# First half of k as fp32 with casts on chip, and one w_out product one slot earlier

## The chip, the cores and the metric

The kernel runs on one core of a Trainium2 chip. The metric is the device time of one execution in microseconds; for several runs the median is given. A profile is one execution, recorded with the start and length of every instruction and of every DMA packet.

## The reference

The input is q, k and v of shape (8, 8, 576, 64) in fp32 (batch, heads, sequence, head dimension), a w_in of 512 x 2048 and a w_out of 2048 x 512.

```
scores = q @ k^T / 8, kept where |i - j| <= 32, else -1e9
attn   = softmax(scores) @ v              # per batch and head
x      = attn as (8*576, 8*64)            # 4608 tokens of 512
h      = x @ w_in
g      = h if h >= 1;  0 if h <= -1;  else (h + 1)^2 / 4
out    = g @ w_out                        # fp32
```

## The kernel before

**Types and layout.** Everything that TensorE (PE) reads is bf16. Almost all loads are issued by GpSimd (POOL), whose DMAs change fp32 to bf16 on the way. The first half of q (`q32`) is the exception: SyncE (SP) and ScalarE (ACT) issue one DMA each for one group of four heads, as fp32, and `cast` (L338) makes bf16 of it on chip: VectorE (DVE) the first 5 of 9 columns of rows (L342), ACT the other 4 (L343), into one tile `qb` with both head groups side by side. `load_half` (L80) loads one half of one of q or k of batch 0 for one group of heads; without an engine given it is POOL's, and a tile `qh` or `kh` in bf16 is the result.

**Attention.** PE transposes q and k to `qT` and `kT`, in parts of five and four columns: a tile from `cast` takes 9 transposes at full width (L189), one from POOL 18 at half width (L187). Part 0 is copied out of PSUM by ACT, part 1 by DVE (L190). `scores` (L211) adds the band's mask by products of an identity with a bias (L206), multiplies blocks of keys with their window of queries (L227) and takes the Exp on ACT (L235). `sums` (L265) multiplies the result with ones and with v (L293); its `end()` takes Ln and Exp(-x) on ACT for the reciprocal (L299, L300), and DVE multiplies into `xT` (L305, for the last 96 tokens of a batch L308).

**The MLP.** Time runs in slots `a` (L482): slot a does 256 tokens (t = a // 8) by 256 columns of w_in (f = a % 8) into one `hp` of PSUM (L504). Tile `hp` has two buffers, and slot 6 takes one of `ps_o`. ACT makes `rr` (L508), then in the slots of `two_on_act` (1 and 7 to 12) also its square (L512), and DVE writes `gT` from hp (L513); in the others DVE does both steps (L515, L516). The products with w_out of the first two blocks of 256 tokens (p = 0, 1) are cut into 16 `pair`s (L452): pair x does half of w_out's columns (x // 8) with 4 of 16 rows of blocks (x % 4) in 16 products of 128 x 256 (L460; 8 for each 128 tokens). Their first ten places are written by hand in the list `pairs` (L378), as (slot, pair); the other parts go by `quarter` (L444), one for each slot.

**The start.** All comes in program order on each engine. POOL issues: the first half of k (two DMAs), an affine_select for the identity and the band (L131), v of batch 0 (four DMAs), w_in in pieces, the second half of q and k, more of w_in with the first part of w_out, three copies for masks, the rest of w_out's first 256 columns (L155: rows of blocks 4 to 7, then 8 to 15), then rows of batch 1 for q and k (`load_rows`), v of batch 1, and so on. PE: 11 products of zeros (`keep_warm`, L336), transposes of q, transposes of k, 3 warm products, three groups of scores, 4 warm products, the first sums, 2, the second sums, 7, then slot 0. ACT and DVE: the casts of q, the copies of qT, the copies of kT, and ACT the Exps. The second half of q and k is transposed in slot 1 (`tposes`, L323), and its scores come in slots 2 and 3.

Of the kernel before, what the change touches and what calls it, by code (L numbers as in the profile page):

```python
# [7 lines left out]
FP = mybir.dt.float32  # L8
# [6 lines left out]
def kernel(  # L15
# [19 lines left out]
    nc = tc.nc  # L35
    B, H, S, D = q.shape
# [40 lines left out]
    qn, kn, vn = {}, {}, {}  # L77
    HD = (slice(0, 64), slice(64, 128))

    def load_half(half, t, h, eng=None, x=None):  # L80

        src, dst, nm = ((q, qn, "qh"), (k, kn, "kh"))[t]
        if (0, half) not in dst:
            dst[0, half] = early.tile([128, 2, S], BF, name=nm, tag=nm, bufs=2) if x is None else x
        (eng or nc.gpsimd).dma_start(out=dst[0, half][:, h], in_=src[0].rearrange(
            "(h y) (l p j) d -> h l p y (j d)", h=2, l=2, p=32)[h][half])
# [29 lines left out]
                            in_=moe_w_out.rearrange("(ko ki) f -> ki ko f", ki=128)[:, k0:k1, 256 * c:256 * c + 256])  # L116

    early = ctx.enter_context(tc.tile_pool(name="early", bufs=1))
    q32 = early.tile([128, 2, S], FP, name="q32")
    for h in range(2):  # L120
        load_half(0, 0, h, (nc.sync, nc.scalar)[h], q32)
    for h in range(2):
        load_half(0, 1, h)
    A.preload_act_table_set("natural_log_exp_and_others")
    warm = const.tile([128, 512], BF, name="warm")
    V.memset(warm, 0.0)
# [15 lines left out]
    def put(todo):  # L142
        for fn, *x in todo:
            fn(*x)
# [7 lines left out]
    for m, n, x in ((mask4, 8, 128), (mask8, 4, TAIL)):  # L152
        P.tensor_copy(m.rearrange("p (n j) -> p n j", n=n),
                      band[:, :x].rearrange("p (n j) -> p n j", n=1).to_broadcast([128, n, x]))
    put([(load_w_out, 0, 4, 8), (load_w_out, 0, 8, 16)] + [(load_rows, 1, t) for t in range(2)])  # L155
    put([(load_v, 1, n) for n in range(4)] + [(load_w_out, 1, 8 * n, 8 * n + 8) for n in range(2)])
    put([(load_nat, 2, t) for t in range(2)] + [(load_v, 2, n) for n in range(4)])

# [3 lines left out]
    def qkT(b, t):  # L162
        if t == 0:
            return qTs[b % 3][:, PAD:]
        if b not in kT:
            kT[b] = ktp.tile([128, NY * S], BF, name="kT")
        return kT[b]

    def tpose(b, n, t, copy, ps):


        half, part = divmod(n, 2)
        j0, j1 = ((0, 5), (5, 9))[part]
        if b:
            src = qn[b] if t == 0 else kn[b]
            src = [src[:, half + 2 * h] for h in range(2)]
            dst = qkT(b, t).rearrange("d (y e p j) -> d y e p j", y=2, e=2, j=9)[:, half, :, :, j0:j1]
            like = "d j (e p) -> d e p j"
        else:
            src = (qn, kn)[t][b, half]  # L180
            src = src if src.shape[1] == 9 else [src[:, h] for h in range(2)]
            dst = qkT(b, t).rearrange("d (y l p j) -> d l y p j", l=2, p=32, j=9)[:, half, :, :, j0:j1]
            like = "d j (p y) -> d y p j"
        for j in range(j0, j1):
            if isinstance(src, list):
                for h in range(2):
                    nc.tensor.transpose(ps[HD[h], j - j0], src[h][:, D * j:D * j + D], ident)  # L187
            else:
                nc.tensor.transpose(ps[:, j - j0], src[:, j], ident)  # L189
        return lambda: copy(dst, ps[:, :j1 - j0].rearrange(like, p=64 if b else 32))  # L190
# [20 lines left out]
    def scores(b, ys, pars, cs, eng, pool=ps_s, w=128):  # L211

        if b not in pt:
            pt[b] = ptp.tile([128, 2, 2, 2, 512], BF, name="pt")
        ps = two_banks(pool)
        n = 0
        if eng is None:
            cols = (ys[1] - ys[0]) * (pars[1] - pars[0]) * (cs[1] - cs[0])
            add_mask([ps[:, h] for h in range(2)], cols, w)
        for y1 in range(*ys):  # L220
            for par in range(*pars):
                for c2 in range(*cs):
                    c = 2 * c2 + par
                    for a in range(2):
                        for h in range(2):
                            s0 = S * (y1 + 2 * a) + 64 * c
                            nc.tensor.matmul(ps[HD[a], h, w * n:w * n + w], kT[b][HD[h], s0:s0 + 64],  # L227
                                             qTs[b % 3][HD[h], PAD + s0 - 32:PAD + s0 - 32 + w],
                                             start=eng is not None, stop=True, skip_group_check=True)
                    n += 1  # L230
        p = pt[b][:, :, ys[0]:ys[1], pars[0]:pars[1], 128 * cs[0]:128 * cs[1] - 128 + w]
        m = 2 if n > cs[1] - cs[0] else 1
        p = p[:, :, ys[0] - ys[0]] if ys[1] - ys[0] == 1 else p[:, :, :, 0]
        like = "p h (y j) -> p h y j"
        A.activation(p, ps[:, :, :w * n].rearrange(like, y=m), AF.Exp, scale=D ** -0.5)  # L235
        mask(eng, p, mask4[:, :256 * n].rearrange("p (h j) -> p h j", h=2).rearrange(like, y=m))
# [81 lines left out]
    def tp1(pool):  # L318
        if pool is ps_h:
            return pool.tile([128, 8, 128], BF, name="tp", tag="hp")  # L320
        return pool.tile([128, 2, 8, 128], BF, name="tp", tag="bb")[:, 0]
# [10 lines left out]
    def keep_warm(n, pool, tag):  # L332

        z = pool.tile([128, 512], FP, name="z", tag=tag)
        for _ in range(n):
            nc.tensor.matmul(z, warm[:, :128], warm, start=True, stop=True)  # L336

    def cast(x, nm, cut):  # L338

        y = early.tile([128, 9, 2, D], BF, name=nm)  # L340
        o, i = y.rearrange("p j h d -> p h j d"), x.rearrange("p h (j d) -> p h j d", d=D)
        V.tensor_copy(o[:, :, :cut], i[:, :, :cut])  # L342
        A.copy(o[:, :, cut:], i[:, :, cut:])  # L343
        return y.rearrange("p j h d -> p j (h d)")

    with tc.tile_pool(name="ps_p", bufs=1, space=bass.MemoryType.PSUM) as ps_p:
        keep_warm(11, ps_h, "hp")

        V.memset(qkT(0, 0).rearrange("d (y s) -> d y s", y=NY)[:, :, S // 2:352], 0.0)
        for b in range(LONG):  # L350
            V.memset(qkT(b, 0).rearrange("d (y s) -> d y s", y=NY)[:, :, S - PAD:], 0.0)
        V.memset(qkT(0, 1).rearrange("d (y s) -> d y s", y=NY)[:, :, S // 2:320], 0.0)
        qn[0, 0] = cast(q32, "qb", 5)
        qq = [tpose(0, n, 0, (A.copy, V.tensor_copy)[n], tp1(ps_h)) for n in range(2)]
        for x in qq:
            x()
        kk = [tpose(0, n, 1, (A.copy, V.tensor_copy)[n], tp1((ps_n, ps_p)[n])) for n in range(2)]
        keep_warm(3, ps_h, "hp")
        for x in kk:
            x()  # L360
        scores(0, (0, 1), (0, 2), (0, 2), None)
        scores(0, (0, 2), (0, 1), (2, 3), None, ps_n, 32)
        scores(0, (1, 2), (0, 2), (0, 2), None, ps_p)
        keep_warm(4, ps_h, "hp")
        e0 = sums(0, 0, 0, TB)
        keep_warm(2, ps_h, "hp")
        e1 = sums(0, 1, 0, TB, ps_p)
        keep_warm(7, ps_h, "hp")
        e0()
        e1()  # L370
# [4 lines left out]

    NB = NT // TB
    NF = DFF // 256
    pairs = [(6, 0), (8, 1), (9, 2), (10, 3), (11, 4), (12, 5), (15, 6), (15, 8), (16, 7), (17, 9)]  # L378
    two_on_act = (1, 7, 8, 9, 10, 11, 12)
    ev = {}  # L380

# [100 lines left out]
    for a in range(NF * NB + NF):  # L482
        t, f = divmod(a, NF)
# [70 lines left out]
```

## Time and profile before

| | us |
|---|---|
| median of 4 runs | 309.04 (308.52 to 309.59) |
| the profiled execution | 308.60 |
| its span (first to last instruction) | 306.8 |
| PE busy | 299.3 (98%) |
| DVE, ACT, POOL busy | 241.9 (79%), 192.4 (63%), 76.8 (25%) |
| chain that ended last: PE's share | 90% |
| fp32 halves of q, issue to landing | 3.6 and 4.3 |
| kh (POOL, 144 KB each), issue to landing, of four | 4.5 to 5.8 |
| granted TensorE clock | full, throughout |

How to read it: a row of the timeline gives start, length, engine, line, what is written and read, and in brackets the idle time of the engine before it with what ended that. The chain of waits is followed back from the last instruction; each piece starts when the piece before it releases it. PEld is the loading of weights, which runs beside PE. DMA packets of POOL are counted by what they write, in bf16.

### The profile page before, as it was taken

What the parts mean: (1) busy time and instruction counts of PE and PEld (TensorE: products, weight loads), DVE (VectorE), ACT (ScalarE), POOL (GpSimd) and SP (SyncE); (2) the same over time, 40 slices, a digit from 0 to 9 for tenths busy, and PEclk for the clock granted to TensorE, in tenths of its full rate; (3) what the DMA queues carried; (4) which work ended last, traced back from release to release, by engine and by line L of the source; (5) the groups of instructions that cost most, each with busy time, mean ns of one, the idle gap of its engine ahead of it and who ended that gap; (6) DMA issues with size and microseconds to landing.
All of it is one profiled execution on the core that took longest, in us unless ns stands there. A gap on an engine that the chain in (4) does not pass through costs nothing.

```text
span 306.8 us, 8495 instructions
## 1 busy us (share of the span) xinstructions
PE 299.3 (98%) x3650; PEld 206.3 (67%) x3650; DVE 241.9 (79%) x376; ACT 192.4 (63%) x320; POOL 76.8 (25%) x91
## 2 busy tenths in 40 slices
PE   7989999999999999999999999999999999999995
PEld 3467878876666666666666666666666666666654
DVE  4278568888888888889888888889888888888760
ACT  4688786738856667666656666566676666554431
POOL 8798451037009106400550002800000000000000
PEclk9999999999999999999999999999999999999999
DMA  9999999999999999996899154990810011010111
GB/s 153 184 197 199 182 201 152 169 156 157 138 191 99 177 172 102 162 93 142 105 167 140 34 112 104 141 157 19 177 49 36 34 36 36 35 36 34 60 45 68
DMA packets 137157, 35.70 MB, mean 116 GB/s; under 512 B 122144, under 2 KB 132896, under 8 KB 137120
## 3 DMA queue, kind: packets, MB, share of 16 engines
q0 software_dynamic: 102960, 18.06, 82.8%
q1 hardware_dynamic: 34016, 16.81, 24.4%
q8 instruction: 28, 0.46, 0.6%
q10 hardware_dynamic: 144, 0.29, 0.4%
q14 instruction: 9, 0.07, 0.1%
HBM read 36.70 MB, written 9.44 MB: 150 GB/s over the span
## 4 chain that ended last, share of the span: by engine, by line
PE 90%; ACT 3%; DVE 2%; DMA 2%; POOL 1%; issue 1%; POOLq 0%; ACTq 0%
PE hp L504 39%; PE op L444 36%; PE bb L293 6%; PE op L460 4%; PE bb L227 2%; DMA vn<-in_v_dram 2%; PE op L433 1%; ACT pt L235 1%; POOL vn L106 1%; PE tp L187 1%; DVE xT L305 1%; ACT rc L300 1%; ACT lr L299 1%; DVE mx L515 0%; ACT rr L508 0%
## 5 line engine op out<-in xcount | busy, mean ns | idle before, releaser
L504 PE MATMUL hp<-xT,w_in 128*128 128x256 bf16 x1152 | 149.6, 273 | 1.5 <-DMA w_in<-in_moe_w_in_dram 0.6
L508 ACT ACTIVATE rr<-hp 128x512 f32<-128x512 f32 x144 | 85.6, 594 | 87.9 <-PE hp L504 87.9
L504 PEld LDWEIGHTS <-w_in 128*128 128x128 bf16 x1152 | 112.0, 98 | 41.2 <-issue 1.6
L444 PE MATMUL op<-w_out,gT 128*128 128x512 bf16 x496 | 126.9, 380 | 0.0
L515 DVE TENSOR_TENSOR mx<-hp,rr 128x512 f32<-128x512 f32 x137 | 94.5, 689 | 30.9 <-ACT rr L508 28.9
L516 DVE SCALAR_TENSOR_TENSOR gT<-rr,mx 128x512 bf16<-128x512 f32 x137 | 95.2, 695 | 4.7
L444 PEld LDWEIGHTS <-gT 128*128 128x128 bf16 x496 | 46.1, 98 | 34.8
L98 POOL DMA_DIRECT2D qn<-in_q_dram x12 | 14.6, 1222 | 113.2 <-DMA kT<-kn 109.5
L235 ACT ACTIVATE pt<-bb 128x1024 bf16<-128x1024 f32 (+1 forms) x33 | 32.7, 1001 | 4.9 <-PE bb L227 3.6
L305 DVE TENSOR_TENSOR xT<-bb,rc 128x512 bf16<-128x512 f32 (+1 forms) x32 | 21.0, 657 | 10.2 <-ACT rc L300 9.7
L106 POOL DMA_DIRECT2D vn<-in_v_dram x32 | 27.5, 900 | 3.4 <-DMA w_out<-in_moe_w_out_dram 3.4
L300 ACT ACTIVATE rc<-lr 128x512 f32<-128x512 f32 (+2 forms) x40 | 23.5, 587 | 1.3
L449 ACT COPY osb<-op 128x512 f32<-128x512 f32 x31 | 18.0, 582 | 8.7 <-PE op L444 8.3
L299 ACT ACTIVATE lr<-bb 128x512 f32<-128x512 f32 (+2 forms) x40 | 22.1, 552 | 0.5 <-PE bb L293 0.4
L201 DVE TENSOR_TENSOR pt<-pt,mask 128x1024 bf16<-128x1024 bf16 (+1 forms) x33 | 20.2, 614 | 0.5 <-ACT pt L235 0.5
L293 PE MATMUL bb<-pt,ones 64*64 64x256 bf16 (+3 forms) x352 | 19.6, 256 | 0.1
L293 PE MATMUL bb<-pt,vn 64*64 64x128 bf16 (+3 forms) x712 | 18.4, 204 | 0.3 <-DMA vn<-in_v_dram 0.3
L293 PEld LDWEIGHTS <-vn 64*64 64x64 bf16 x712 | 16.7, 107 | 0.5 <-DMA vn<-in_v_dram 0.5
L460 PE MATMUL op<-w_out,gT 128*128 128x256 bf16 x128 | 16.5, 273 | 0.0
L293 PEld LDWEIGHTS <-ones 64*64 64x64 bf16 x352 | 10.2, 105 | 8.9 <-issue 8.9
L98 POOL DMA_DIRECT2D kn<-in_k_dram x12 | 14.6, 1232 | 0.6 <-DMA vn<-in_v_dram 0.3
L227 PE MATMUL bb<-qT,kT 64*64 64x128 bf16 (+1 forms) x520 | 13.1, 217 | 0.2 <-DVE kT L190 0.2
(59 smaller groups left out, 113.1 us busy)
## 6 DMA issues: line engine op xcount, KB each, us to landing
out_dram<-osb SPq DMA_DIRECT2D x35, 256.0 KB, 2.4
vn<-in_v_dram POOLq DMA_DIRECT2D x32, 144.0 KB, 10.5
qn<-in_q_dram POOLq DMA_DIRECT2D x12, 288.0 KB, 6.8
kn<-in_k_dram POOLq DMA_DIRECT2D x12, 288.0 KB, 9.4
w_in<-in_moe_w_in_dram POOLq DMA_DIRECT2D x12, 128.0 KB, 5.8
w_out<-in_moe_w_out_dram POOLq DMA_DIRECT2D x3, 512.0 KB, 15.2
kh<-in_k_dram POOLq DMA_DIRECT2D x4, 144.0 KB, 5.1
qn<-in_q_dram POOLq DMA_DIRECT2D x1, 576.0 KB, 9.6
```

The source lines that it names most:

```text
L98: nc.gpsimd.dma_start(out=x[:, :, h], in_=src[b, NY * h:NY * h + NY].rearrange("y s d -> (y s) d") .rearrange("(u p) d -> p u d", p=128))
L106: nc.gpsimd.dma_start(out=vn[b][64 * a:64 * a + 64, :, h], in_=v[b, y:y + 2].rearrange("y s d -> (y s) d") .rearrange("(c r) d -> r c d", ...
L235: A.activation(p, ps[:, :, :w * n].rearrange(like, y=m), AF.Exp, scale=D ** -0.5)
L293: nc.tensor.matmul(bb[HD[h], a, o + c0:o + c1], ones[HD[a]] if c is None else vn[b][HD[a], c, h], p(a, h), start=n == 0, stop=True, skip_g ...
L299: A.activation(lr[:, :, :D0], bb[:, :, D0:2 * D0], AF.Ln)
L300: A.activation(rc[:, :, :D0], lr[:, :, :D0], AF.Exp, scale=-1.0)
L444: nc.tensor.matmul(o, gT[tt // 2][:, j, 128 * (tt % 2):128 * (tt % 2) + 128], w_out[:, j], start=not done, stop=len(done) == 2 * NF - 1, s ...
L460: nc.tensor.matmul(o[:, tt], gT[p][:, j, 128 * tt:128 * tt + 128], w_out[:, j, 256 * half:256 * half + 256], start=not done, stop=len(done ...
L504: nc.tensor.matmul(hp[:, j], w_in[:, kk, 256 * f + 128 * j:256 * f + 128 * j + 128], xT[:, kk, r0:r0 + TB], start=n == 0, stop=n == 3)
L508: A.activation(rr, hp, AF.Relu, scale=0.5, bias=0.5)
L515: V.tensor_max(mx, hp, rr)
L516: V.scalar_tensor_tensor(g, rr, 1.0, mx, op0=ALU.min, op1=ALU.mult)
```

## The change

- The first half of k comes as q does: fp32, one DMA from SP and one from ACT, behind those of q in their queues, into a new tile `k32`. POOL's two issues of `kh` at the head of its queue are gone (those of the second half stay).
- `cast(k32, "kb", 5)` follows the cast of q and stands before the copies of qT in the order of ACT and DVE: one more cast on each. The transposes of this half become 9 at full width.
- The rest of w_out's first columns is loaded in pieces of 4, 4 and 4 rows of blocks instead of 4 and 8.
- Pair 1 moves from slot 8 to slot 7, so that it comes on PE before the products of slot 8 instead of behind them.

Nothing else moves in the order of any engine.

```diff
     early = ctx.enter_context(tc.tile_pool(name="early", bufs=1))
-    q32 = early.tile([128, 2, S], FP, name="q32")
-    for h in range(2):
-        load_half(0, 0, h, (nc.sync, nc.scalar)[h], q32)
-    for h in range(2):
-        load_half(0, 1, h)
+    q32, k32 = [early.tile([128, 2, S], FP, name=nm) for nm in ("q32", "k32")]
+    for t, x in enumerate((q32, k32)):
+        for h in range(2):
+            load_half(0, t, h, (nc.sync, nc.scalar)[h], x)
...
-    put([(load_w_out, 0, 4, 8), (load_w_out, 0, 8, 16)] + [(load_rows, 1, t) for t in range(2)])
+    put([(load_w_out, 0, k, k + 4) for k in range(4, 16, 4)] + [(load_rows, 1, t) for t in range(2)])
...
         qn[0, 0] = cast(q32, "qb", 5)
+        kn[0, 0] = cast(k32, "kb", 5)
         qq = [tpose(0, n, 0, (A.copy, V.tensor_copy)[n], tp1(ps_h)) for n in range(2)]
...
-    pairs = [(6, 0), (8, 1), (9, 2), (10, 3), (11, 4), (12, 5), (15, 6), (15, 8), (16, 7), (17, 9)]
+    pairs = [(6, 0), (7, 1), (9, 2), (10, 3), (11, 4), (12, 5), (15, 6), (15, 8), (16, 7), (17, 9)]
```

## The prediction

> **What bounds the kernel now.** I read the page's engine shares first, then PE's waits, then the chain of waits over the first 45 us, then the timeline of the first 9 us. The page says how little there is to win:
>
> ```profile
> PE 299.3 (98%) x3650; PEld 206.3 (67%) x3650; DVE 241.9 (79%) x376; ACT 192.4 (63%) x320; POOL 76.8 (25%) x91
> PEclk9999999999999999999999999999999999999999
> ```
>
> TensorE (PE) is busy for 98% of the span at the full clock. All its waits lie in the first 28.5 us (engine, line, what it waited for; total, times, longest):
>
> ```profile
> PE z L336 <- DVE warm L126: 1.2, 1, 1.2
> PE tp L189 <- DVE qb L342: 0.8, 1, 0.8
> PE hp L504 <- DMA w_in<-in_moe_w_in_dram: 0.6, 1, 0.6
> PE hp L504 <- DVE xT L305: 0.4, 1, 0.4
> PE hp L504 <- DVE xT L308: 0.4, 1, 0.4
> PE bb L293 <- DMA vn<-in_v_dram: 0.3, 1, 0.3
> PE bb L227 <- DVE kT L190: 0.2, 1, 0.2
> ```
>
> After 28.44 us PE is the bound. So the end moves by as much as the chain up to there moves, and the chain (start, length, what) is this:
>
> ```profile
> 1.96 0.57 POOL kh L85
> ...
> 3.03 2.46 POOL vn L106 x3
> 5.49 5.21 DMA vn<-in_v_dram
> 10.70 0.04 issue
> 10.74 0.52 PE bb L293 x17
> 11.27 0.02 issue
> 11.29 0.61 ACT lr L299
> ...
> 27.83 0.56 DVE xT L308
> 28.39 0.04 issue
> 28.44 1.03 PE hp L504 x8
> ```
>
> From 10.74 us on every step follows the one before within 0.04 us, over ACT (Ln, Exp), DVE (xT), PE (the first w_in products), ACT, DVE (the second tposes copies), the scores at 19.69, ACT, DVE. There is no slack in it: a shift S of the sums at 10.74 arrives whole at 28.4. The 0.6 us for w_in (18.11 us) is not on it; it is slack of PE alone. What stands ahead of 10.74 is v's landing; the rival start is the scores. They go by this piece of the timeline (start, length):
>
> ```profile
> 5.12 0.62 ACT L343 CAST qb<-q 128x512 bf16<-128x512 f32 x1 [2.44 <-DMA q<-in_q_dram]
> 5.14 0.71 DVE L342 CAST qb<-q 128x640 bf16<-128x640 f32 x1 [1.07 <-DMA q<-in_q_dram]
> 6.39 0.76 ACT L190 COPY qT<-tp 128x640 bf16<-128x640 bf16 x1 [0.66 <-PE tp L189]
> 6.62 0.73 DVE L190 COPY qT<-tp 128x512 bf16<-128x512 bf16 x1 [0.77 <-PE tp L189]
> ```
>
> q32 lands for casts at 5.12, qT is copied, then kT (ACT to 7.93, DVE 7.39 to 8.12), the scores start at 8.24, their Exps run from 8.73 to 10.84, and the first sums start at 10.12 without a wait. They stop only at the last part of v, for 0.28 us.
>
> **The change, part by part.**
>
> *When k lands.* This decides the case. The trace's records of DMA packets show q as 256 packets of 2,304 bytes: ScalarE's half from 2.15 to 3.98 us, SyncE's from 3.25 to 4.74, median 93 ns each. SyncE's first packet starts 6 ns after ScalarE's half ended on its first engine (3.239): each of the 16 engines works through one half, then the other. The casts start 0.38 us after the last packet. k as fp32 is 256 such packets again, 16 for each engine, 16 x 93 ns = 1.49 us. Behind q it ends at 4.74 + 1.49 = 6.23, and its casts start at t = 6.61. It would be no earlier unless the slow first packets of q (1.09 us for eight on the first engine, against 0.74) leave room that k fills: at best 0.35 us less, t = 6.26. If v's packets come between, it is later: that is rival 1.
>
> *The casts.* Both engines cast k before they copy qT. The gaps before those copies (0.66 us on ACT, 0.77 on DVE) would hide casts of 0.62 and 0.71 us if k were there at 5.85. It isn't. So DVE: kb from 6.61 to 7.32, qT (0.73) to 8.05, kT (0.73) to 8.78, with some 0.03 us of gaps 8.81. ACT: 0.62 + 0.76 + 0.76 from 6.61 gives 8.75. PE: the nine transposes of kb (0.68, as for qb) are done by 8.07, before kT's copy needs them; the three warm products (0.82) end by 8.9, and the masks' products start some 0.07 us ahead of their end, as they do now. kT is complete at 8.81 in place of 8.12: the scores, the Exps and the four warm products shift by 0.69, say 0.70.
>
> *What of it is covered.* The sums then start at 10.82 instead of 10.12, and the 0.28 us wait for v goes, if v lands by then. Shift of the chain: S = 0.70 - 0.28 = **+0.42 us**. ACT is in time for the Ln: its third Exp ends at 10.84 + 0.70 = 11.54, before 11.29 + 0.42 = 11.71.
>
> *What leaves POOL.* Two issues of kh, 1.26 us. The affine_select, which waited for them to 2.59, can follow step's memset (ends 1.41), so v's four issues start at about 1.8 in place of 2.94. This gives v no earlier landing: v's packets follow k on the engines in both versions (now 5.46 to 10.27 us), and k costs an engine 16 x 93 = 1.49 us against 16 x 107 = 1.71 for kh, 0.2 us at most. Later loads gain nothing: POOL already stands waiting for old DMAs (0.25 us at 9.64, 1.00 at 14.49), and the DMA row is full up to 60 us. At worst v lands 0.2 later and still before 10.82 + 0.62, when its last part is used.
>
> *What SyncE and ScalarE get.* One issue each, 0.66 and 0.63 us. SyncE's next work is an output at 34.94. ScalarE's table load moves from 1.40 to 2.03 and ends at 3.31; the engine then waits to 5.12. Cost nothing; without that idle time, 0.63.
>
> *Transposes.* 18 of half width (0.85 us) become 9 (0.68). That is 0.17 us less on PE while it waits for copies: nothing. DVE's and ACT's added casts are the terms above.
>
> *The split of w_out.* One issue more on POOL, 0.77 us at 23.5. Everything behind it in POOL's queue (load_rows of q and k, v, w_out's other half) is issued that much later, up to v's last at 28.4, where a backlog of transfers is already waiting: v's packets, issued from 25.01, run from 34.5 on. Cost 0; if the backlog were gone, 0.77 on tiles first used at 34.8. Columns 0, j 4 to 7 finish at 26.2 by the packet records, before slot 7 needs them.
>
> *Pair 1 from slot 8 to 7.* PE would do its 0.87 to 1.04 us from 28.04, when slot 7's products end, and so fill the 0.41 us wait for xT. But slot 9's hp takes slot 7's buffer, which DVE's L513 gives back at 30.31; DVE is busy 6.09 of the 6.30 us before 30.40. In the trace slot 9 starts at 30.36, at once when pair 1 ends and when the buffer comes free. Filling one only opens a gap of 0.25 us ahead of slot 9: gain 0 (bounds: 0.41 gained if DVE has slack, 0.1 lost if slot 8's products, now last before slot 9, make its ACT and DVE work late). I take 0, because DVE's busy row speaks against slack.
>
> *Sum.* The profiled execution took 308.6 us, 1.8 above its span of 306.8: 308.6 + 0.42 = 309.0. The four runs have a median of 309.04, 0.4 above this one, so for the median I say 309.04 + 0.42 = 309.5, rounded up.
>
> *A rule against the change.* Where a hardware-queue transfer meets a backlog of POOL's 128-byte packets, this trace shows it waiting for the backlog: the output issued at 34.94 moved its first packet 4.26 us later, behind 4,033 of v's, while the one at 64.37 with nothing beside it took 0.75. The Trainium skill, page "DMA: Bandwidth & Descriptors", section "Queues, rings and completion order", says otherwise: an engine takes turns among its queues, a packet of up to 64 descriptors each. By that page, my estimate is one or two of v's turns (64 of its 288 descriptors in 4.8 us are 1.07 us) inside k: 1.1 to 2.1 us later, the sum 310.6 to 311.6. By the measured wait it is first come first served, and then k is safe as long as it arrives first.
>
> **Rivals.**
> 1. *v gets ahead of k (slower).* Place: the DMA engines at 3.7 to 4 us. POOL's first packets came 1.92 us after their issue on idle engines (66.35 to 68.27), so v can arrive at 1.8 + 1.9 = 3.7; k, issued at 1.37 and 1.40, arrives between 0.75 us later (the output at 64.37) and 2.5 (SyncE's q half, 0.74 to 3.25), at 2.1 to 3.9. It decides if k's second half arrives after 3.7. One of v's four loads ahead of k costs 72 x 16.7 ns = 1.2 us: S = 1.6, 310.7. Three or all of them cost the 4 us of the outputs: S = 4.4, 313.5, with v then in time. For it: the ranges overlap. Against: q's SyncE half was held up by ScalarE's packets, not by its own issue.
> 2. *k comes in time.* If t is 5.9, the casts fit the gaps, and only v's 0.28 us is left to be gained, if v comes 0.3 sooner: 308.8. Against it: 93 ns a packet leaves no room.
> 3. *The pair's 0.41 us is kept* besides the forecast: 309.04 + 0.42 - 0.41 = 309.05. Against it: L513 at 30.31.
> 4. *The change does not do what it says:* k off POOL frees 1.26 us that no one waits for, and nothing moves: 309.0, the same as 3 in time.
>
> **How the numbers follow.** Forecast (309.1 to 309.9): 0.50. Rival 1: 0.22, of which 0.16 near 310.7 and 0.06 at 312 or more. Rival 2: 0.13. Rivals 3 and 4: 0.15. The range 308.6 to 310.8 reaches from just under rival 2 to the near part of rival 1 and leaves out the far part. The bound for faster or slower is 0.3% (0.93 us, about what a measurement of this kernel can tell from no change). Faster needs under 308.1, which no case gives: 0.06, half of rival 2's chance, for errors in its terms. Slower needs over 309.97: rival 1, 0.22. The rest, 0.72, is no change.
>
> **What would show it.** Right: kb's casts start near 6.6; qT's copies follow at 7.2 to 7.4; the scores start near 8.9; no wait of L293 for vn; slot 9's first product at 30.8. Rival 1: casts after 7.5 with 128-byte packets among k's. Rival 2: casts by 6.0 and Exps from 8.7. Pair: L504 waits ahead of slot 9 for L513 instead of ahead of slot 8 for xT. I am wrong if the chain after 10.8 has slack, or if the end moves without the start.

## The result, and the profile after

The changed kernel took 309.29 us in the median (43 runs, 308.82 to 311.68), the kernel before 308.89 in the same comparison (64 runs). The ratio is **1.0016, 95% interval 1.0009 to 1.0024**: by the ratio 0.16% or 0.5 us slower, by the two medians 0.40 us. The forecast was 309.5 and +0.42 us.

The profiled execution of the changed kernel took 311.42 us, 2.1 us above its median, so it is not the ordinary one. That turned out to be the most instructive thing about it. Its page (busy time of the engines; granted clock and DMA in 40 slices):

```profile
span 309.6 us, 8484 instructions
...
PE 301.1 (97%) x3641; PEld 207.3 (67%) x3641; DVE 242.0 (78%) x377; ACT 192.7 (62%) x321; POOL 75.7 (24%) x90
...
PEclk9799999999999999999999999999999999999999
```

PE is busy 1.8 us longer with 9 products fewer, and the second slice (7.7 to 15.5 us) has a 7 in the clock's row where the kernel before has a 9. What PE waits for:

```profile
PE tp L188 <- DVE kb L341: 1.9, 1, 1.9
PE z L335 <- DVE warm L125: 1.2, 1, 1.2
PE bb L205 <- DVE qT L189: 0.6, 1, 0.6
PE hp L504 <- DVE gT L513: 0.6, 1, 0.6
PE hp L504 <- DVE xT L304: 0.4, 1, 0.4
```

(Lines between the loads and the slots are one lower than before: L305 is L304, L308 is L307.) The waits for v, for w_in and for the last tokens' xT are gone. In their place stand a wait of 1.9 us for k's cast, one of 0.6 us of the masks' products (L205), and one of 0.6 us for gT, ahead of slot 9. The head of the chain of waits (start, length, what) has k where it had v:

```profile
0.74 0.65 ACTq L85
1.40 0.03 issue
1.43 6.46 DMA k<-in_k_dram
7.89 0.02 issue
7.91 0.50 DVE kb L341
8.42 0.02 issue
8.44 0.76 ACT qT L189
9.20 0.04 issue
9.24 1.28 PE z L335 x3
```

So in this execution k's casts began at 7.91 us. Its packet records show why: all but ten of k's 256 packets were done by 6.04, and the last ten came one after the other up to 7.00, 0.09 us apart, as a single DMA engine works them off. That engine keeps the usual pace, so it must have been behind already; the records don't name the engines, so they don't show since when. The table puts the start beside the end for the kernel before and for every profile that has k's first half from SyncE and ScalarE right ahead of v; "last packet" is the end of the last of the 2,304-byte packets, "Ln" the start of the first Ln on ACT.

| kernel | k's last packet | casts of kb | Ln | span | execution |
|---|---|---|---|---|---|
| before (no kb) | - | - | 11.29 | 306.8 | 308.60 |
| e4, v issued later | 5.94 | 6.62 | 11.43 | 306.9 | 308.68 |
| e9, PE filled | 6.30 | 6.93 | 11.74 | 307.1 | 308.87 |
| e10, filled and v later | 6.16 | 7.08 | 11.98 | 307.3 | 309.10 |
| e2, k only | 6.56 | 7.26 | 12.07 | 307.4 | 309.24 |
| e7, PE filled with five | 6.52 | 7.07 | 12.15 | 307.5 | 309.29 |
| e1, the change again | 6.20 | 7.24 | 13.40 | 308.9 | 310.68 |
| the change | 7.00 | 7.91 | 14.28 | 309.6 | 311.42 |

Against the kernel before, the span goes with the first Ln, less 0.0 to 0.2 us: 0.14 later there is 0.1 later at the end, 0.45 is 0.3, 0.78 is 0.6, 2.99 is 2.8. That is the prediction's main claim (no slack from 10.7 to 28.4, PE the bound after) in seven points, each a single execution. But between the casts of kb and the Ln, e2 and e1 differ by 1.3 us with the same casts. That is the clock.

### The profile page after: what moved, and what is told of

Same layout as the page of the kernel before. It is cut to its first block, busy times and chain, and to the rows that moved or that the text cites. A ratio compares the mean times of both kernels' runs of the same rounds, so it can differ in the third digit from the quotient of the medians.

```text
span 309.6 us, 8484 instructions
## 1 busy us (share of the span) xinstructions
PE 301.1 (97%) x3641; PEld 207.3 (67%) x3641; DVE 242.0 (78%) x377; ACT 192.7 (62%) x321; POOL 75.7 (24%) x90
## 4 chain that ended last, share of the span: by engine, by line
PE 90%; ACT 3%; DVE 2%; DMA 2%; issue 1%; ACTq 0%
PE hp L504 39%; PE op L444 36%; PE bb L292 6%; PE op L460 4%; PE bb L226 3%; DMA k<-in_k_dram 2%; PE op L433 1%; ACT pt L234 1%; PE z L335 1%; PE tp L186 1%; DVE xT L304 1%; ACT rc L299 1%; DVE mx L515 1%; ACT lr L298 1%; PE bb L205 0%
## 5 line engine op out<-in xcount | busy, mean ns | idle before, releaser
L304 DVE TENSOR_TENSOR xT<-bb,rc 128x512 bf16<-128x512 f32 (+1 forms) x32 | 21.0, 657 | 11.5 <-ACT rc L299 10.9
```

## Experiments

**e1, the change again.** No edit.

> The changed kernel once more, with nothing edited. The profile of it that I have is of an execution at 311.4 us, 2.1 above the median of 309.29: there k's casts start at 7.91 us, because one of the 16 DMA engines finished its part of k 1.1 us after the other fifteen. My theory (k lands behind q at the DMA engines' pace, t = 6.6 us) expects of an ordinary execution: casts of kb between 6.4 and 6.9, first scores near 8.9, slot 9's first product near 30.8, ratio 1.001 to 1.002. The rival (the end moves by something other than the start) expects casts of kb by 6.0 or the scores at 8.3 and the same time.

Measured: 12 runs, median 309.80, 308.89 to 313.8, ratio 1.0025 (1.0006 to 1.0045), above the 1.001 to 1.002 expected. Its profile is once more of an execution above 310 (310.68). Its casts of kb begin at 7.24, later than the 6.4 to 6.9 expected. The granted clock by stages (stretch, its length, then busy time and count for PE, PEld, DVE, ACT, POOL, then the clock, DMA share, GB/s):

```profile
7.00:8.00 1.00, 0.20 (x3) 0.20 (x4) 0.75 (x2) 0.76 (x2) 0.90 (x2) 0.97 3.54 135
8.00:9.00 1.00, 1.00 (x10) 0.79 (x8) 0.49 (x2) 1.00 (x2) 0.36 (x1) 0.50 3.95 118
9.00:10.00 1.00, 1.00 (x3) 0.15 (x1) 0.61 (x1) 0.21 (x1) 0.39 (x2) 0.50 2.60 152
10.00:11.00 1.00, 1.00 (x29) 0.70 (x32) 0.00 (x0) 0.00 (x0) 0.82 (x2) 0.50 1.65 186
11.00:12.00 1.00, 1.00 (x42) 0.61 (x31) 0.00 (x0) 0.82 (x1) 0.88 (x3) 0.82 1.46 195
```

The clock is at one half from 7.94 (0.97 of the stretch before 8) to 11.36 (0.82 after 11): 3.4 us. The profile of the change has the same from 9.4 to 12.8. In both, the three warm products, the masks and the scores run meanwhile, and take up to twice as long: in e1 1.49 us instead of 0.81 for the warm products. Of the 44 executions of the change that list a clock, five have a mean of 0.993 or 0.994, and they are just those above 310 (310.90 to 311.68); the other 39 lie at 0.998 to 1.000 and 308.82 to 309.79, median 309.23. In e1 it is five of 12 (310.51 to 313.8, clock 0.989 to 0.994); a sixth is above 310 without it (310.20 at 0.999). The 75 executions of the kernel before that were run beside the experiments all have 0.998 or more. For the ordinary execution, which the expectation is about, e2 and e4 have the profiles.

**e2, k only.**

```diff
-    pairs = [(6, 0), (7, 1), (9, 2), ...
+    pairs = [(6, 0), (8, 1), (9, 2), ...
-    put([(load_w_out, 0, k, k + 4) for k in range(4, 16, 4)] + ...
+    put([(load_w_out, 0, 4, 8), (load_w_out, 0, 8, 16)] + ...
```

> The change without its pair and without the split of w_out: pair 1 in slot 8, w_out as 4 and 8 blocks. If k's landing is the whole cost, as I forecast, this has the ratio of the whole change, 1.0010 to 1.0020, and PE waits for xT ahead of slot 8's products again. If the pair's move gave back its 0.41 us in the change, this one is slower by 0.4 us than the whole change: 1.0025 to 1.0035.

Measured: 12 runs, median 309.29, ratio 1.0020 (0.9998 to 1.0042; one run at 312.75 with the clock at 0.995, the others to 309.52). k's path alone has the cost of the whole change; a gain by the pair is not seen, though the interval alone would not exclude it. PE waits for xT ahead of slot 8 again, for 0.2 us. Its profile is of an ordinary execution (309.24, clock 1.0). Timeline of ACT, DVE and PE:

```profile
5.28 0.62 ACT L342 CAST qb<-q 128x512 bf16<-128x512 f32 x1 [1.93 <-DMA q<-in_q_dram]
7.26 0.62 ACT L342 CAST kb<-k 128x512 bf16<-128x512 f32 x1 [1.37 <-DMA k<-in_k_dram]
7.27 0.49 DVE L341 CAST kb<-k 128x640 bf16<-128x640 f32 x1 [1.49 <-DMA k<-in_k_dram]
7.68 0.72 DVE L189 COPY qT<-tp 128x512 bf16<-128x512 bf16 x1
7.82 0.68 PE L188 MATMUL tp<-ident,kb 128*128 128x128 bf16 x9 [1.31 <-DVE kb L341]
8.54 0.73 DVE L189 COPY kT<-tp 128x512 bf16<-128x512 bf16 x1
10.01 2.11 ACT L234 ACTIVATE pt<-bb 128x1024 bf16<-128x1024 f32 x3 [0.83 <-PE bb L226]
12.07 0.60 ACT L298 ACTIVATE lr<-bb 128x512 f32<-128x512 f32 x1
```

This is the prediction's paragraph on the casts, step by step, only 0.65 us later: the casts first, then both copies, the Exps 1.28 later than before (8.73), the Ln 0.78 later (11.29).

**e3, pair and split only.** The kernel before with the two edits of e2 turned round.

```diff
-    pairs = [(6, 0), (8, 1), (9, 2), ...
+    pairs = [(6, 0), (7, 1), (9, 2), ...
-    put([(load_w_out, 0, 4, 8), (load_w_out, 0, 8, 16)] + ...
+    put([(load_w_out, 0, k, k + 4) for k in range(4, 16, 4)] + ...
```

> The kernel before with only the pair moved to slot 7 and w_out split in 4, 4, 4; k by GpSimd as before. My theory: nothing, 0.9997 to 1.0003, because slot 9's products wait for the buffer that L513 of slot 7 gives back; PE's wait moves from slot 8 (for xT) to slot 9 (for gT). The rival (PE keeps the 0.41 us): 0.9985 to 0.9990.

Measured: 12 runs, median 308.79, ratio 0.9996 (0.9984 to 1.0009), span 306.7. PE's waits from 15 us on:

```profile
PE hp L504 <- DMA w_in<-in_moe_w_in_dram: 0.8, 2, 0.6
PE hp L504 <- DVE gT L513: 0.5, 1, 0.5
PE tp L187 <- DMA kh<-in_k_dram: 0.3, 1, 0.3
```

The wait for L308's xT ahead of slot 8 (0.4) is gone, and a wait for L513 ahead of slot 9 (0.5) is there. Slot 9 starts at 30.29, 0.07 before the 30.36 of the kernel before, and the span is 0.1 shorter (306.7 and 306.8). The gap moved; it was not filled.

**e4, v later.** The change, with GpSimd held up for 0.9 us before v's issues.

```diff
+    idle = early.tile([128, 1024], BF, name="idle")
+    P.memset(idle, 0.0)
     for n in range(4):
         load_v(0, n)
```

> The whole change, with a memset of an unused tile of 128 x 1024 on GpSimd before v's four loads, so that v is issued about as late as in the kernel before (near 2.8 us instead of 1.84). First come, first served: k is ahead of v anyway, so k lands when it does in e1_same (within 0.2 us), and the time is that of e1_same or up to 0.2 us more. Turns (v's packets between k's): k lands 0.3 to 1 us earlier than in e1_same, and the time falls by as much, to a ratio under 1.0005.

Measured: 12 runs, median 309.20, ratio 1.0022 (0.9997 to 1.0046), two runs at 311.8 and 312.4 with the clock at 0.994 and 0.993. v's issue moved from 1.84 to 2.73 us, but its first packet came at 5.49 as in the others (5.55 to 5.67): it waits its turn behind k in either case. The one profile has k's casts at 6.62, the earliest of all and 0.62 ahead of e1's, which by itself is the second theory's sign. But the median did not fall under 1.0005 as that theory has it, and e10 repeats the delay with casts at 7.08. So 6.62 is more likely this execution's luck, and v's place seems to cost k nothing here; one profile of each kernel shows no more.

**e5, k behind v.**

```diff
-    for t, x in enumerate((q32, k32)):
-        for h in range(2):
-            load_half(0, t, h, (nc.sync, nc.scalar)[h], x)
+    for h in range(2):
+        load_half(0, 0, h, (nc.sync, nc.scalar)[h], q32)
...
     V.tensor_scalar(bias, band, ...)
+    V.memset(k32, 0.0)
+    for h in range(2):
+        load_half(0, 1, h, (nc.sync, nc.scalar)[h], k32)
```

> The whole change, but k's two loads are issued only after a memset of k32 on DVE (near 3.5 to 4 us), so that v's first packets are on the DMA engines before them. This measures the price of rival 1 of the prediction. First come, first served: k's packets wait for most of v's flood, its casts start at 9.5 to 11.5 us, and the time is 2.5 to 5 us over the kernel before. Turns between the queues: k's casts start by 8.5 and the time is at most 2.5 us over it.

Measured: four runs, 314.67 to 316.24, ratio 1.0209 (1.0187 to 1.0232), 6.4 us over the kernel before, more than either theory gave. All four have the clock at 0.989. k's issue and casts:

```profile
3.80 0.54 SPq L85 DMA_DIRECT2D k<-in_k_dram  x1
3.80 0.58 ACTq L85 DMA_DIRECT2D k<-in_k_dram  x1
4.81 0.62 ACT L344 CAST qb<-q 128x512 bf16<-128x512 f32 x1 [2.10 <-DMA q<-in_q_dram]
11.10 0.62 ACT L344 CAST kb<-k 128x512 bf16<-128x512 f32 x1 [5.67 <-DMA k<-in_k_dram]
```

The casts came when the first theory has them, but the packets show no first come, first served to the end. v's first came at 3.98. SyncE's k began at 5.41, behind 1,210 of v's 4,608, ScalarE's at 6.78, behind 2,165; from there k's packets ran among v's and ended at 10.13, the last of them begun with 692 of v's still to come. From issue to first packet that is 1.61 and 2.98 us. The two halves of q, issued in the same way at 0.74 onto idle DMA engines, took 1.43 and 2.28 (first packets at 2.17 and 3.02). So behind v's flood k's start came only some 0.2 to 0.7 us later, an estimate from this one execution, and from then on k's packets shared the engines with v's. Whether SyncE's half first let the one load of v (1,152 packets) pass that was ahead of it, the run doesn't tell. k is also issued 2.4 us later here than in the change (3.80 against 1.40).

**e6, v in rows.** The kernel before, v of batch 0 in eight DMAs, one for each group and row of heads, the rows of the first sums first.

```diff
-    for n in range(4):
-        load_v(0, n)
+    for y1 in range(2):
+        for n in range(4):
+            load_v_row(0, n, y1)      # heads NY*h + 2*a + y1: nine chunks of 64 rows
```

> The kernel before, with v of batch 0 loaded in eight parts instead of four, the heads that the first sums need first. If v's landing is what bounds the start of the kernel before (its chain of waits says so), the wait of the sums for v goes, the first Ln starts at 10.8 instead of 11.3, and the time falls by 0.3 to 0.5 us: ratio 0.9983 to 0.9992. The rival (the start doesn't set the end, or something else is late at once): 0.9995 to 1.0010.

Measured: six runs, 310.96 to 312.82, ratio 1.0089 (1.0068 to 1.0109). The rival was right about the end:

```profile
2.94 5.90 POOL L113 DMA_DIRECT2D vn<-in_v_dram  x8
8.76 2.54 POOL L117 DMA_DIRECT2D w_in<-in_moe_w_in_dram  x4
10.67 0.60 ACT L307 ACTIVATE lr<-bb 128x512 f32<-128x512 f32 x1
12.30 0.28 PE L301 MATMUL bb<-pt,vn 64*64 64x96 bf16 x8 [0.88 <-DMA vn<-in_v_dram]
```

The first Ln did come 0.62 us earlier (10.67), so v's landing did bound it. But eight issues take POOL 5.90 us in place of 3.43 (0.74 each for half the bytes, against 0.86), w_in is issued 2.4 us later, the second sums wait for v, and products of the first slots for w_in (three waits, 1.4 us in all). Three of the six runs (311.65 to 312.82) have the clock at 0.994, although k comes by GpSimd here: the clock falls in other kernels than the change, too. The profile is of a run without it.

**e7, five products of zeros in the gap.**

```diff
+        keep_warm(5, ps_s, "bb")
         kk = [tpose(0, n, 1, ...) for n in range(2)]
```

> The whole change, with five more products of zeros on PE between the transposes of q and those of k, where PE waits for k's casts (1.3 to 1.9 us in the three profiles so far). In two of those profiles the granted clock then falls to 0.50 for some 3.4 us, and those executions are 1.5 to 2.4 us slower than the others. My theory: PE's emptiness while it waits for k causes this; with the wait filled no execution is over 310 us, the clock is 1.00 throughout, and the median is at 0.3 to 0.5 us over the kernel before (1.0010 to 1.0016). The rival (the clock falls for some other reason, or the slow executions come from the DMA alone): some executions over 310 us remain, as in e1_same.

Measured: 12 runs, median 308.97, **308.85 to 309.29**, ratio 0.9996 (0.9984 to 1.0009). None is above 310; the median is under the 1.0010 expected. The same stages as e1's:

```profile
7.00:8.00 1.00, 1.00 (x6) 0.39 (x4) 0.93 (x2) 0.94 (x2) 0.82 (x2) 1.00 3.11 145
8.00:9.00 1.00, 1.00 (x13) 0.70 (x11) 0.45 (x2) 0.81 (x2) 0.23 (x1) 1.00 3.76 124
9.00:10.00 1.00, 1.00 (x38) 0.52 (x40) 0.48 (x1) 0.28 (x1) 0.35 (x2) 1.00 2.47 154
10.00:11.00 1.00, 1.00 (x39) 0.60 (x27) 0.00 (x0) 0.91 (x1) 0.88 (x2) 1.00 1.55 190
```

From 7.11 on, where the clock opened in this execution, PE is full and the clock stays at 1.00. The interval does not tell this kernel from the one before.

**e8, v far behind k.** e4's edit with four memsets.

> The whole change with four memsets of an unused tile on GpSimd before v's loads, so that v's packets reach the DMA engines at about 7.5 us, long after k's. k's casts started 0.7 to 1.0 us after the last packet of k so far, q's 0.35 us after the last of q. If the flood of v's 128-byte packets right behind k makes k's completion late, k's casts here start 0.35 to 0.45 us after its last packet, at 6.3 to 6.7 us. If the two loads on each queue are the reason, the 0.7 to 1.0 us stay. v comes some 2 us later, and the sums wait for it: 1 to 2 us over the kernel before in either case.

Measured: six runs, median 313.57, 311.04 to 314.19, ratio 1.0155 (1.0134 to 1.0177), more than expected; four of the six have the clock at 0.989 to 0.995. v's first packet came at 7.43. k's last ended at 6.24 and its casts began at 6.75, 0.51 us later; q's gap in the same execution is 0.51 (4.80 to 5.31), too. With v close behind, k's gap was 0.55 (e7), 0.63 (e9), 0.68 (e4), 0.70 (e2), 0.91 (the change), 0.93 (e10) and 1.04 (e1). 0.51 lies under all of them, as v's flood as the cause would have it, but 0.55 is so near that one execution does not settle it.

**e9, three products in the gap.** e7's edit with 3 for 5.

> The whole change with three products of zeros between the transposes of q and of k, not five. Five ran to 8.2 us, 0.65 us past the end of DVE's cast of k (7.56), and so delayed the transposes of k. My theory (the empty PE lets the clock fall, and each delay of kT goes whole into the end): three products end by 7.7, the clock stays at 1.00, no execution is over 310 us, and the median is 0.2 to 0.5 us under that of e7_fill, so ratio 0.9980 to 0.9995. The rival (three are too few to hold the clock): some executions over 310 us come back.

Measured: 12 runs, median 309.06, 308.66 to 309.71, ratio 1.0003 (0.9991 to 1.0014), all clocks 0.998 or more. The products end by 7.28, before DVE's cast of kb does (7.52), and kT is complete at 9.02 instead of 9.48. That gain of 0.46 us in the one profile, of which 0.14 is k's earlier casts (6.93 and 7.07), is 0.4 at the end (spans 307.1 and 307.5), but the medians don't show it. Three are enough to hold the clock; the gain in the median was a miss.

**e10, three products and v later.** e9 with e4's memset.

> As e9_fill3, with v's loads 0.9 us later by one memset on GpSimd, as in e4_v_later. There k's casts started at 6.62 us, against 7.07 to 7.26 in three profiles with v at 1.84. If v's earlier issue holds k up, the casts start by 6.7 here too, and the time is 0.3 to 0.5 us under e9_fill3's. If 6.62 was only that execution's luck, the casts start between 6.6 and 7.3, and the time is e9_fill3's within 0.2 us.

Measured: 12 runs, median 309.12, 308.64 to 309.28, ratio 0.9999 (0.9987 to 1.0011); k's casts at 7.08. v's later issue brings nothing. In all, 36 executions with the gap filled have no fall of the clock, against 13 of 80 with it open (the change 5 of 44, e1 5 of 12, e2 1 of 12, e4 2 of 12). With the landing of k or v moved far back it is more: e5 4 of 4, e8 4 of 6. No version tried beats the kernel before.

## Why the prediction was right, and what it missed

*The direction, the size and the place* were right: k lands later than it did by GpSimd, the scores follow, v's wait covers a part, and the rest arrives at the end. Step by step:

- **k's last packet, 6.23 forecast:** 5.94 to 6.56 in the ordinary executions. Right; the packets' pace of 93 ns sets it, but for the profile of the change (7.00).
- **From the last packet to the casts, 0.38:** mis-sized. It is 0.55 to 1.04 for k, 0.35 to 0.51 for q. So t was 6.62 to 7.26 and not 6.61. Whether v's packets, which follow k's on the same engines, make its completion late stays open (e8).
- **From the casts to kT, 2.20:** 2.01 in e2, 2.07 in e4, 2.09 in e9. DVE's cast of kb took 0.49 to 0.58 us in these, where the one row of before had 0.71 for q.
- **The cover by v's wait, 0.28:** mis-sized. The shift of the Exps less the shift of the Ln is 1.28 - 0.78 in e2, 0.64 - 0.14 in e4, 0.95 - 0.45 in e9: 0.50 each time. I took PE's row for the wait; the row of the weight loads beside it, in the kernel before, shows a stop of 0.48 us (10.26 to 10.74), which fits the 0.50:

```profile
10.74 0.18 PEld L293 LDWEIGHTS <-vn 64*64 64x64 bf16 x9 [0.48 <-DMA vn<-in_v_dram]
10.74 0.28 PE L293 MATMUL bb<-pt,vn 64*64 64x96 bf16 x8 [0.28 <-DMA vn<-in_v_dram]
```

- **The sum:** the shift forecast at the scores was 0.70 and is 0.64 to 1.28, the cover 0.28 and is 0.50, so that S is 0.14 (e4), 0.45 (e9) or 0.78 (e2) against 0.42. The two wrong sizes offset each other, and that the forecast of 0.42 came so near is in part luck. The median of the 39 executions without a fall of the clock, 309.23, is 0.34 over the before of its comparison.
- **No slack to 28.4 us:** right, by the table. Slot 9 starts at 30.81 in e9 and 31.14 in e2, 0.45 and 0.78 late, just as the Ln; after that 0.15 to 0.2 us is given back on the way to the end, which I have not traced.
- **The pair and the split, 0:** right, and by the mechanism named (e3).
- **v's earlier issue, 0:** right. v's first packet came at 5.55, 3.7 us after its issue, and at 5.46 in the kernel before: the earlier issue brought no earlier landing.
- **Rival 1, v ahead of k:** didn't happen in any profile of the change; its price was probably too low. e5 gives 6 us for k behind v, where the prediction had 1.6 to 4.4; but k is issued 2.4 us later there, and the clock falls as well (0.989), so 6 us is more than rival 1 alone. The prediction's reading of the outputs, first come, first served, does not hold for k: the output waited 4.26 us behind v's packets, but k in e5 got in 0.2 to 0.7 us later than q on idle engines and then shared. Why the two differ stays open. The Trainium skill's page "DMA: Bandwidth & Descriptors", section "Queues, rings and completion order", has each engine take turns among its queues; k in e5 agrees with that, and so do the last ten packets of k in the profile of the change, which alternate one by one between SyncE's queue and ScalarE's, while the output's 4.26 us does not.
- **The clock:** missed altogether. The prediction said that PE is at full clock and left it there; it priced the wait for k by what runs after it, and not by what the wait does to PE. In 13 of 80 executions this costs some 2 us more in the change (310.9 to 311.7, beside 309.23), and more in some of e1, e2 and e4 (up to 313.8). In the profiled one it is about half of the 2.8 us: its Ln is 2.99 us later than before, e2's 0.78 with casts 0.65 us earlier, which leaves some 1.6 us to the clock; in e1, with e2's casts, it is 1.33.

## The clock of TensorE

The first products of zeros show when the clock opens, for they start 0.43 us apart while it is at half, and 0.21 when it is full. Of e1 and then of the change:

```profile
1.20 4.18 PE L335 MATMUL z<-warm 128*128 128x512 bf16 x11 [1.20 <-DVE warm L125]
1.20 4.88 PE L335 MATMUL z<-warm 128*128 128x512 bf16 x11 [1.20 <-DVE warm L125]
```

In e1 some eight of the eleven are at the slow pace, so the clock opened near 4.55. It fell at 7.94 and came back at 11.36: three edges, 3.4 us apart. In the profile of the change all eleven are slow, so it opened after 5.9, and it fell at 9.4 and came back at 12.8. The clock row shows 1.00 up to the fall, although the first products ran at half pace: it knows of no clock before the first change. In the kernel before, too, the clock is full only from 4.05 us on. The clock records of the traces give the edges to the nanosecond. The first one lies between 4.05 and 7.11 us in the twelve profiles, and every stretch at one clock from there to the end of the kernel lasts 1, 2, 87, 88 or 89 times 3.413 us. So the clock is decided anew every 3.413 us, at a point which differs from one execution to the next.

What decides is how busy PE was in the 3.413 us before. The stretches with the least work, and the first one of some other executions, each in the profile alone:

| execution | stretch, us | PE busy, us | clock in the next |
|---|---|---|---|
| e5 | 5.41 to 8.82 | 1.00 | falls to half |
| e5 | 8.82 to 12.23 | 0.52 | stays at half |
| the change | 6.02 to 9.43 | 1.46 | falls to half |
| e1 | 4.53 to 7.94 | 1.66 | falls to half |
| e2 | 5.54 to 8.95 | 2.02 | stays full |
| e10 | 4.65 to 8.07 | 2.31 | stays full |
| e8 | 5.25 to 8.67 | 2.42 | stays full |
| e4 | 5.03 to 8.44 | 2.44 | stays full |
| before | 4.05 to 7.46 | 2.64 | stays full |

All other whole stretches of the twelve profiles, over a thousand, have 2.1 us or more, and the clock is full after each. So the limit lies between 1.66 and 2.02 us of 3.41. The transposes are counted in these figures, and without them the order is lost: e1 fell with 0.84 us of other work, and e2 did not with 0.69. Where the stretch happens to begin then tells executions apart: e1 and e2 have k's casts at 7.24 and 7.26, their stretches begin at 4.53 and 5.54, and only e1 fell.

The Trainium skill, page "TensorE: Matmul & The Clock Gate", section "Part 1: The HAM clock gate (the "warmup" mystery)", has a free-running window of 4096 cycles, 3.4 us, at whose end the clock is set to half or full; the edges here agree. Its rule of thumb, in section "HAM oscillation — how this bites in real kernels", is to avoid idle gaps of more than about 3.4 us. Here the measurement differs: gaps of 1.38 us (e1) and 1.85 us (the change), with transposes on both sides, were enough.

## What to carry to other kernels

A load that is moved to a faster queue is not there sooner if the DMA engines are full; count the packets ahead of it, and allow for its completion coming later than its last packet, by 0.5 to 1.0 us here. A wait on TensorE has a second price besides its length: where it leaves a 3.4 us stretch half empty, the clock may fall in some executions and not in others, which a median hides and a single profile exaggerates; three products of zeros in the gap removed this (no fall in 24 executions of e9 and e10). And before reading causes from one profile, hold its time against the median of the runs.

## What the runs showed of the hardware that I had not expected

- POOL's issue of a DMA costs nearly the same for half the descriptors: 0.74 us for 576 packets of v, 0.86 for 1,152 (e6 and before).
- A hardware-queue transfer that arrived behind POOL's flood began only 0.2 to 0.7 us later than one on idle engines, and then shared the engines with it (e5).
- TensorE's clock was decided every 3.413 us by the work of the 3.413 us before: half after 1.66 us or less, full after 2.02 or more (twelve profiles).
- DVE's cast of 640 fp32 columns took 0.49 to 0.93 us in these profiles, with the same instruction and operands; what sets it was not tried.
- One DMA engine can end 1 us after the others (the profile of the change, 7.00 and 6.04 at most), and nothing that depends on the tile starts before it. Why it was late is open.
